# Block-sparse attention: the scores of two heads in one product of 128 rows and 64 columns, queries in five zeroed places read with a stride, heads dealt out anew

## The chip, the cores and the metric

The kernel runs on one core of a Trainium2 chip, as one launch. The metric is the device time of that launch in microseconds (us), the median of several runs. The profile beside it is one execution, recorded by the hardware profiler. In its rows PE is TensorE (matmuls), PEld is TensorE loading the stationary operand of a matmul, DVE is VectorE, ACT is ScalarE, POOL is GpSimd, SP is SyncE, which here only issues transfers (DMAs). A name with a q behind it (SPq, ACTq) is that engine's sequencer. L334 is line 334 of the kernel.

## The reference, cut to what matters

Four batches, eight heads, 768 positions in 24 blocks of 32, 64 numbers a head. All is float32.

```python
scores = (q @ k.T) / 8                     # per batch and head
mask   = |block_i - block_j| <= 1          # the window
mask  |= block_i in (0, 23) or block_j in (0, 23)
mask  |= block_j in sampled_blocks[block_i]   # 3 random blocks for each row of blocks
attn   = softmax(where(mask, scores, -1e9))
x      = attn @ v                          # (4, 768, 512), heads side by side
theta  = x @ w_theta
y      = w_tok_r @ (x * cos(theta)) + w_tok_i @ (x * sin(theta))   # over positions
u      = x + y
out    = u + relu(u @ w_ch)
```

The three sampled blocks are an input and known only at run time.

## The kernel before, in words

**Two stages.** `attention` works through 56 units; `token_mix` (called `follow`) is the rest of the reference, and starts inside the last steps of attention. The change touches attention alone.

**Units.** The batches go in two pairs (`bp`), and one unit handles the 16 heads of a pair (2 batches of 8 heads) for one block of 32 queries. For each pair there are six wide units (`"w"`), which do the first and the last block of queries against all keys, and 22 inner units (blocks 1 to 22), each against eight blocks of 32 keys: the window, the first and last block and the three sampled ones, gathered in `kgs` (keys) and in `vas`, `vbs` (values). So there are 44 inner units.

**A unit's stages**, each a function:

- `scores` (S): products of queries (stationary) and keys (moving) into two PSUM banks, then a VectorE minimum over each row (`m`, L337; the scale is -1/8, so that the minimum is the maximum of the scores). In an inner unit these are 16 products, one a head (L334): each takes 64 rows of the array (the numbers of one head) and 32 columns (its 32 queries), with 256 keys streaming. The head's index is dealt out as `e` (which half of the 128 rows, 2), `p` (which 32 of the 128 columns, 4) and `b` (the batch, 2). Every float32 product is two matmuls with two loads of the stationary operand in the trace, so an inner unit shows 32 matmuls S and 32 loads.
- `weights` (P): four exponentials on ScalarE (L354).
- `turn` (T): eight 128x128 transposes on TensorE (L364); `evict` (pT) copies them to SBUF on ScalarE (L370).
- `values` (X): 32 products of 128 rows and 32 columns with 65 columns of values streaming (the 65th is a column of ones and gives the sum), 64 matmuls in the trace (L388); in a wide unit half as many, of 64 columns (X_w).
- `finish` (DVE): division by the sum; `store` writes two units' outputs to DRAM (`xs`). For wide units `join` (POOL) and `joined` combine the three parts and write them with four DMAs each (L432).

**Order.** It is written out by hand (`tc.manual_schedule()`): in step n each engine gets its instructions in this order: scores(n+1), the keys of n+3 (POOL and ACT: `gather_window`, `gather_keys`, `gather_key`), a share of decoding the token mix's weights (`Decoder`, mostly DVE), turn(n), values(n-1), evict(n), weights(n+1), scale of the queries of n+3 (`scale_q`, ACT), finish(n-1), then the transfers: `load_q` for n+6 (SP), `gather_values` for n+2 (POOL, an indirect DMA, L308), `load_window` for n+1 (SP, and a POOL copy, L299), `store` (SP). TensorE's order in a step is therefore S(n+1), T(n), X(n-1). Queues are worked in order.

**Queries.** `load_q` fetches two units' queries with one DMA of 256 KB into one of four rotating tiles; `scale_q` scales both at once on ScalarE (L239, 512 numbers a row). The decoder's pieces are 512 or 576 numbers wide.

**Heads.** On the host `rows_by_head` puts the two halves `e` of a batch's heads in the upper and lower 64 rows.

Of the kernel before, what the change touches and what calls it, by code (L numbers as in the profile page):

```python
# [10 lines left out]
F32 = mybir.dt.float32  # L11
# [8 lines left out]
P = 128  # L20
NB = 24
NP = 2
ZEROS = float(768 * NP)
Q_BUFS = 4
VB = 4


# [148 lines left out]
def attention(tc, qT, qE, kT, vr, sampled, xs, ident, early_pieces, late_pieces, first_place, follow, spares):  # L176
# [10 lines left out]

    nc = tc.nc  # L190
    with ExitStack() as ctx, ExitStack() as early:

# [6 lines left out]
        qp = ctx.enter_context(tc.tile_pool(name="qp", bufs=1))  # L199
# [10 lines left out]
        ks, wide, qbs, qes, unscaled, st, numbers = {}, {}, {}, {}, {}, {}, {}  # L210
# [15 lines left out]
        def load_wide(bp, t, queue=nc.sync):  # L226
            for c in (2 * t, 2 * t + 1):
                queue.dma_start(wide[bp][c], vr[768 * bp + 128 * c : 768 * bp + 128 * c + 128])

        def load_q(bp, i):  # L230
            if i % 2 == 0:
                return
            t = qp.tile([P, 2, 2, 4, 32], F32, tag="q", name=f"q{bp}_{i}", bufs=Q_BUFS)
            nc.sync.dma_start(t.rearrange("r u b p f -> r u (b p f)"), qT[bp][:, i - 1 : i + 1, :])
            qbs[bp, i], qbs[bp, i + 1] = t[:, 0], t[:, 1]
            unscaled[bp, i] = t.rearrange("r u b p f -> r (u b p f)")

        def scale(tile_):
            nc.scalar.mul(tile_, tile_, -0.125)  # L239

        def scale_q(bp, i):
            if (bp, i) in unscaled:
                scale(unscaled.pop((bp, i)))

        def scale_edges(bp):
            scale(qes[bp].rearrange("r b p f -> r (b p f)"))
# [68 lines left out]
        def scores(unit):  # L315

            bp, i, x = unit
            s = st[unit] = {}
            sc = ps_s[units.index(unit) % 2].tile([P, 2, 2, 256], F32, tag="S", name=f"S{name(unit)}")
            heads = [(b, p, e) for b in range(2) for p in range(4) for e in range(2)]  # L320
            if i == "w":
                t, a = x
                q, keys = qes[bp], ks[bp][:, 8 * t : 8 * t + 8]
                for b, s_, e in [(b, p, e) for b, p, e in heads if p < 2]:
                    rows, p = slice(64 * e, 64 * e + 64), 2 * a + s_
                    nc.tensor.matmul(sc[64 * s_ : 64 * s_ + 64, e, b, :], q[rows, b, p, :], keys[rows, :, 4 * b + p, :], start=True, stop=True)
                if t == 0:
                    mxs[a] = wp.tile([P, 3, 4], F32, tag="mx", name=f"mx{name(unit)}")
                m = mxs[a][:, t]
            else:  # L330
                q, keys = qbs.pop((bp, i)), kgs[i % 2]
                for b, p, e in heads:
                    rows = slice(64 * e, 64 * e + 64)
                    nc.tensor.matmul(sc[32 * p : 32 * p + 32, e, b, :], q[rows, b, p, :], keys[rows, :, 4 * b + p, :], start=True, stop=True)  # L334
# [38 lines left out]
        def values(unit):  # L373
            bp, i, x = unit
            s = st[unit]
            s["X"] = ps_x.tile([P, 2, 2, 65], F32, tag="X", name=f"X{name(unit)}")
            if i == "w":
                t, a = x
                parts, width = [(wide[bp][2 * t + c], 128) for c in range(2)], 64
            else:  # L380
                parts = [(vas[i % 2], 96 if i == 1 else 128), (vbs[(i + 1) % VB], 96 if i == NB - 2 else 128)]
                a, width = 0, 32
            for b in range(2):
                for e in range(2):
                    for c, (v, rows) in enumerate(parts):
                        for w_ in range(128 // width):
                            rr, v0 = slice(width * w_, width * w_ + width), 260 * (2 * b + e) + 65 * (2 * a + w_)
                            nc.tensor.matmul(  # L388
                                s["X"][rr, b, e, :], s["T"][0:rows, 4 * c + 2 * e + b, rr], v[0:rows, v0 : v0 + 65], start=c == 0, stop=c == 1,
                            )  # L390
# [35 lines left out]
        def joined(bp, a):  # L426
            xe = wp.tile([P, 2, 2, 2, 64], F32, tag="xo", name=f"xe{bp}_{a}", bufs=2)[:, 0]
            normalised(f"{bp}_a{a}", xws[a][:, 0], xe)
            for s_ in range(2):
                for z in range(2):  # L430
                    r0, p0 = 64 * s_ + 32 * z, 32 * (2 * a + s_)
                    nc.sync.dma_start(xs[bp, p0 : p0 + 32, (NB - 1) * z].rearrange("r b c -> r (b c)"), xe[r0 : r0 + 32].rearrange("r b e d -> r (b e d)"))  # L432

        mxs, fs, xws, xos = {}, {}, {}, {}
        units = []
# [16 lines left out]

        spares.append(lambda: qp.tile([P, 4, 4, 32], F32, tag="q", name=f"spare{len(spares)}", bufs=Q_BUFS))
        with tc.manual_schedule():
            tab = Tables(nc, cp, sampled)
            load_edges(0)
            make_places(0)
            load_k(0, 0, 8)  # L460

# [5 lines left out]
            for t in range(1, 3):  # L467
                load_k(0, 8 * t, 8)
                load_wide(0, t)
                decoder.load(t - 1, nc.sync)  # L470
                load_q(0, 2 * t - 1)
            make_places(1)
            scale_edges(0)
            do(0, scores)
            do(0, weights)
            steps = len(units) + 1
            for n in range(steps):
# [338 lines left out]
def sparse_attention_then_token_mix(ctx, tc, qT, qE, kT, vr, sampled, w_theta, w_tok_r, w_tok_i, w_ch, outT):  # L816
    nc = tc.nc
    n_batch = outT.shape[0]
# [3 lines left out]
    bias = []  # L822
# [4 lines left out]
    xs = dram.tile([NP, P, NB, 2, P], F32, name="xs")  # L827
# [25 lines left out]
    def pieces(name, f0, f1, f, tiles):  # L853


        def piece(c):
            parts = lambda: [t[:, c - f0 : c - f0 + f] for t in tiles()]
            return Piece(nc, parts, words[name][:, 2 * c : 2 * (c + f)], f"{name}_{c}")
# [10 lines left out]
    late = pieces("tok_r", 2304, 4608, 576, chunks(second, 0, 3)) + pieces("tok_i", 0, 3072, 512, chunks(second, 3, 4))  # L869
# [5 lines left out]
    follow = token_mix(tc, w, last, xs, outT, bias, n_batch, lambda: spares[0]())  # L875
# [50 lines left out]
```

## Time and profile before

| | us |
|---|---|
| three runs | 613.40, 607.53, 612.38 |
| their median | 612.38 |
| the profiled execution: its own time | 617.04 |
| the profiled execution: span from first to last instruction | 615.3 |
| mean granted TensorE clock in it | 0.969 |

A row of the timeline reads: start (us from the span's start), duration, engine, line, operation, output <- input, shape (rows x columns of the array, then the operand), count, and in brackets how long the engine was idle before and what ended it. In the chain of work that ended last a row reads: start, duration, what; "issue" is time in which the engine waited for nothing that the profile shows. A row of the stretches reads: from:to, length, then busy time and number of instructions of PE, PEld, DVE, ACT and POOL, the granted clock, the DMA engines' busy share and GB/s.

### The profile page before, as it was taken

The page shows a single profiled execution, that of the slowest core. Times are in us where ns is not written, and L with a number is a line of the kernel's source. Part 1 is how long each engine was busy: PE and PEld are TensorE (multiplying, and loading weights), DVE is VectorE, ACT ScalarE, POOL GpSimd, SP SyncE. Part 2 cuts the span into 40 slices and gives each one's busy share as a digit, 9 for nine tenths or more (in the row PEclk, how much of TensorE's full clock was granted, in tenths as well). Part 3 has the DMA queues.
Part 4 walks back from the last instruction along what each step waited for, and adds up shares of the span by engine and source line. Part 5 has one row for each costly group of instructions (what it writes and reads, how often), then busy time and mean ns, then how long its engine had stood idle before and what let it go on. Part 6 is the DMA issues. An engine that isn't in the chain of part 4 may idle for free.

```text
span 615.3 us, 17294 instructions
## 1 busy us (share of the span) xinstructions
PE 554.5 (90%) x7072; PEld 437.4 (71%) x7072; DVE 424.5 (69%) x845; ACT 336.2 (55%) x684; POOL 176.4 (29%) x280
## 2 busy tenths in 40 slices
PE   3988769779978886999999997999999999999997
PEld 1755546557645554678888886888888888888886
DVE  5589657768898999787999996456852548723252
ACT  2887658758948877775656553143740446520220
POOL 1399666643596677450000010000000000000000
PEclk9999789998979999999999998999999999999999
DMA  8979996877888889662323132311212210112002
GB/s 307 325 173 258 254 259 203 252 213 256 250 222 231 251 216 269 180 170 85 105 84 105 49 86 69 105 35 34 64 40 78 79 51 22 37 39 77 1 0 103
DMA packets 53199, 86.67 MB, mean 141 GB/s; under 512 B 5504, under 2 KB 31744, under 8 KB 52736
## 3 DMA queue, kind: packets, MB, share of 16 engines
q1 hardware_dynamic: 43440, 54.27, 29.1%
q0 software_dynamic: 6688, 21.78, 13.4%
q10 hardware_dynamic: 2992, 9.51, 5.3%
q8 instruction: 56, 0.92, 0.6%
q14 instruction: 23, 0.19, 0.1%
HBM read 72.95 MB, written 12.58 MB: 139 GB/s over the span
## 4 chain that ended last, share of the span: by engine, by line
PE 64%; DVE 12%; DMA 9%; issue 7%; ACT 6%; SPq 1%; POOL 1%; DVEq 0%; ACTq 0%; POOLq 0%
PE ya L654 14%; PE X L388 8%; PE S L334 7%; PE yb L654 7%; PE T L364 6%; DMA va<-in_vr_dram 5%; PE o L681 2%; PE h L595 2%; PE o L683 2%; PE h L598 2%; PE h L596 2%; PE o L682 2%; PE T_w L364 2%; PE X_w L388 2%; ACT zh L636 2%
## 5 line engine op out<-in xcount | busy, mean ns | idle before, releaser
L654 PE MATMUL ya<-w_second,zh 128*128 128x512 f32 x288 | 107.1, 396 | 0.0
L654 PE MATMUL yb<-w_second,zh 128*128 128x256 f32 x288 | 80.5, 279 | 0.0
L334 PE MATMUL S<-kg,q 64*32 64x256 f32 x1408 | 62.5, 407 | 14.0 <-issue 13.8
L354 ACT ACTIVATE P<-S,m 128x256 f32<-128x256 f32 x176 | 69.6, 492 | 6.7 <-DVE m L337 6.4
L370 ACT COPY pT<-T 128x512 f32<-128x512 f32 x88 | 47.6, 593 | 37.3 <-PE T L364 37.0
L337 DVE TENSOR_REDUCE m<-S 128x4 f32<-128x1024 f32 x44 | 53.7, 1220 | 19.1 <-PE S L334 15.1
L388 PE MATMUL X<-vb,pT 128*32 128x65 f32 (+1 forms) x1408 | 55.6, 231 | 10.7 <-issue 10.0
L654 PEld LDWEIGHTS ya<-w_second,zh 128*128 128x128 f32 x288 | 54.1, 188 | 14.0
L388 PE MATMUL X<-va,pT 128*32 128x65 f32 (+1 forms) x1408 | 50.7, 233 | 11.5 <-issue 6.6
L364 PEld LDWEIGHTS T<-ident,P 128*128 128x128 f32 x352 | 40.9, 148 | 27.2 <-issue 10.7
L364 PE MATMUL T<-ident,P 128*128 128x128 f32 x352 | 55.0, 296 | 4.2 <-issue 3.9
L654 PE MATMUL ya<-w_second,zl 128*128 128x512 f32 x144 | 58.0, 403 | 0.0
L654 PEld LDWEIGHTS yb<-w_second,zh 128*128 128x128 f32 x288 | 54.4, 189 | 0.4
L388 PEld LDWEIGHTS X<-vb,pT 128*32 128x32 f32 (+1 forms) x1408 | 40.3, 117 | 15.8 <-issue 15.7
L388 PEld LDWEIGHTS X<-va,pT 128*32 128x32 f32 (+1 forms) x1408 | 35.7, 115 | 20.6 <-issue 13.8
L334 PEld LDWEIGHTS S<-kg,q 64*32 64x32 f32 x1408 | 25.7, 111 | 32.4 <-issue 24.8
L308 POOL DMA_INDIRECT vb<-in_vr_dram,rows x44 | 43.6, 991 | 17.0 <-PE X_w L388 9.3
L611 DVE SCALAR_TENSOR_TENSOR rr<-t,h 128x512 f32<-128x512 f32 x24 | 16.5, 687 | 36.6 <-ACT t L605 36.6
L654 PE MATMUL yb<-w_second,zl 128*128 128x256 f32 x144 | 40.9, 284 | 0.0
L689 DVE SCALAR_TENSOR_TENSOR of<-o,xT 128x512 f32<-128x512 f32 (+1 forms) x24 | 13.2, 557 | 39.1 <-PE o L683 35.7
L299 POOL COPY va<-va 32x1040 f32<-32x1040 f32 (+1 forms) x28 | 30.4, 1086 | 33.7 <-DMA va<-in_vr_dram 16.2
L595 PE MATMUL h<-w_theta_hi,xh 128*128 128x512 f32 x96 | 38.3, 399 | 0.4 <-ACT xh L584 0.4
(167 smaller groups left out, 1320.2 us busy)
## 6 DMA issues: line engine op xcount, KB each, us to landing
va<-in_vr_dram SPq DMA_DIRECT2D x58, 130.0 KB
q<-in_qT_dram SPq DMA_DIRECT2D x22, 256.0 KB
xs<-xo SPq DMA_DIRECT2D x22, 256.0 KB
xr<-xs SPq DMA_DIRECT2D x22, 256.0 KB
xa<-xs SPq DMA_DIRECT2D x88, 64.0 KB
raw_tok_r<-in_w_tok_r_dram ACTq DMA_DIRECT2D x8, 576.0 KB
out_dram<-of SPq DMA_DIRECT2D x16, 256.0 KB
kv<-in_vr_dram SPq DMA_DIRECT2D x6, 520.0 KB
```

The costliest lines, as they stand in the source:

```text
L299: nc.gpsimd.tensor_copy(va[rows], vas[(i + 1) % 2][rows])
L308: nc.gpsimd.indirect_dma_start(out=vb[0:96], out_offset=None, in_=vr, in_offset=bass.IndirectOffsetOnAxis(ap=tab.rows[:, bp, i : i + 1], a ...
L334: nc.tensor.matmul(sc[32 * p : 32 * p + 32, e, b, :], q[rows, b, p, :], keys[rows, :, 4 * b + p, :], start=True, stop=True)
L337: nc.vector.tensor_reduce(m.rearrange("r (e b) -> r e b", e=2), sc, axis=AX.X, op=ALU.min)
L354: nc.scalar.activation(pt[:, e, b], sc[:, e, b], AF.Exp, bias=m[:, 2 * e + b : 2 * e + b + 1], scale=-1.0)
L364: nc.tensor.transpose(banks[k // 4][:, k % 4], pt[:, (k // 2) % 2, k % 2, 128 * (k // 4) : 128 * (k // 4) + 128], ident)
L370: nc.scalar.copy(out[:, 4 * h : 4 * h + 4], bank)
L388: nc.tensor.matmul(s["X"][rr, b, e, :], s["T"][0:rows, 4 * c + 2 * e + b, rr], v[0:rows, v0 : v0 + 65], start=c == 0, stop=c == 1,)
L595: nc.tensor.matmul(ps, hi[:, c, :], wh[:, c, :], start=c == 0, stop=False)
L611: nc.vector.scalar_tensor_tensor(r, t, -C1, ps, op0=ALU.mult, op1=ALU.add)
L654: nc.tensor.matmul(acc, z[:, dd], wt[:, t0 : t0 + n], start=first and (n == 512 or c % 2 == 0), stop=last, skip_group_check=n == 256,)
L689: nc.vector.scalar_tensor_tensor(o, ps, 0.0, xT[b][:, e : e + groups, t0 : t0 + n], op0=ALU.max, op1=ALU.add)
```

## The change

An inner unit's 16 products of 64 rows and 32 columns become eight of 128 rows and 64 columns, two heads each. The stationary operand holds the two heads' queries block-diagonally: head 0 of the two in the upper 64 rows and the first 32 columns, head 1 in the lower 64 rows and the last 32 columns, zeros elsewhere. For that the queries lie in five fixed places `qs` of 128 x (2, 32, 8) numbers, zeroed once at the start by POOL; a load writes only the non-zero halves (two DMAs of 64 KB for each unit, instead of one of 256 KB for two units), and the stationary operand of a product is read from it with a step of eight numbers. The scale goes over the whole place, so there is one for each unit instead of one for two. The queries of unit n+5 are loaded in step n instead of those of n+6. Keys, the values' products, transposes and exponentials keep their shapes; the heads are dealt out in another order (`r`, which 64 columns, is now outside `s`, which half of the rows), so the joined outputs of the wide units need eight DMAs instead of four. The decoder's pieces of 576 become pieces of 512 with a shorter last one (two pieces more). Two of the five places later serve as the two spare tiles of the token mix, which before came from the rotating ones.

```diff
-Q_BUFS = 4
+NQ = 5
...
+        qs = [qp.tile([P, 2, 32, 8], F32, name=f"q{x}") for x in range(NQ)]
...
+        def q_place(bp, i):
+            return qs[((NB - 2) * bp + i - 1) % NQ]
+
         def load_q(bp, i):
-            if i % 2 == 0:
-                return
-            t = qp.tile([P, 2, 2, 4, 32], F32, tag="q", name=f"q{bp}_{i}", bufs=Q_BUFS)
-            nc.sync.dma_start(t.rearrange("r u b p f -> r u (b p f)"), qT[bp][:, i - 1 : i + 1, :])
...
+            t = q_place(bp, i).rearrange("r s f h -> r s (f h)")
+            for s in range(2):
+                rows = slice(64 * s, 64 * s + 64)
+                nc.sync.dma_start(t[rows, s], qT[bp][rows, i - 1])
...
         def scale_q(bp, i):
-            if (bp, i) in unscaled:
-                scale(unscaled.pop((bp, i)))
+            scale(q_place(bp, i).rearrange("r s f h -> r (s f h)"))
...
-                q, keys = qbs.pop((bp, i)), kgs[i % 2]
-                for b, p, e in heads:
-                    rows = slice(64 * e, 64 * e + 64)
-                    nc.tensor.matmul(sc[32 * p : 32 * p + 32, e, b, :], q[rows, b, p, :], keys[rows, :, 4 * b + p, :], start=True, stop=True)
+                q, keys = q_place(bp, i).rearrange("r s f h -> r h (s f)"), kgs[i % 2]
+                for b, e, r in [(b, e, r) for b in range(2) for e in range(2) for r in range(2)]:
+                    h = 4 * b + 2 * e + r
+                    nc.tensor.matmul(sc[64 * r : 64 * r + 64, e, b, :], q[:, h, :], keys[:, :, h, :], start=True, stop=True)
...
-            for s_ in range(2):
+            for r in range(2):
                 for z in range(2):
-                    r0, p0 = 64 * s_ + 32 * z, 32 * (2 * a + s_)
-                    nc.sync.dma_start(xs[bp, p0 : p0 + 32, (NB - 1) * z].rearrange("r b c -> r (b c)"), xe[r0 : r0 + 32].rearrange("r b e d -> r (b e d)"))
+                    out = xs[bp, 64 * r : 64 * r + 64, (NB - 1) * z, :, 64 * a : 64 * a + 64].rearrange("(s q) b d -> q s b d", s=2)
+                    rows = slice(64 * r + 32 * z, 64 * r + 32 * z + 32)
+                    for s in range(2):
+                        nc.sync.dma_start(out[:, s], xe[rows, :, s])
...
             load_edges(0)
+            for t in qs:
+                nc.gpsimd.memset(t, 0.0)
             make_places(0)
...
                 load_q(0, 2 * t - 1)
+                load_q(0, 2 * t)
...
-                if units[min(n + 6, steps - 2)][:2] not in ((0, 1), (0, 3)):
-                    inner(n + 6, load_q)
+                if units[min(n + 5, steps - 2)][:2] not in [(0, i) for i in range(1, 5)]:
+                    inner(n + 5, load_q)
...
-    early = pieces("theta", 0, 2048, 512, all_of("theta")) + pieces("tok_r", 0, 2304, 576, chunks(lambda: first, 0, 3))
+    early = pieces("theta", 0, 2048, 512, all_of("theta")) + pieces("tok_r", 0, 2304, 512, chunks(lambda: first, 0, 3))
...
-        return np.asarray(a).reshape(NP, 2, 2, 4, NB, 32, 64).transpose(0, 2, 6, 4, 1, 3, 5)
+        return np.asarray(a).reshape(NP, 2, 4, 2, NB, 32, 64).transpose(0, 3, 6, 4, 1, 2, 5)
```

More of the change, by code (lines that the diff above doesn't have):

```diff
@@ L209, in attention @@
         vbs = [gp.tile([P, 1040], F32, name=f"vb{x}") for x in range(VB)]
-        ks, wide, qbs, qes, unscaled, st, numbers = {}, {}, {}, {}, {}, {}, {}
+        qs = [qp.tile([P, 2, 32, 8], F32, name=f"q{x}") for x in range(NQ)]
+        ks, wide, qes, st, numbers = {}, {}, {}, {}, {}
         def make_places(bp):
@@ L228, in load_wide @@
                 queue.dma_start(wide[bp][c], vr[768 * bp + 128 * c : 768 * bp + 128 * c + 128])
+        def q_place(bp, i):
+            return qs[((NB - 2) * bp + i - 1) % NQ]
         def load_q(bp, i):
-            if i % 2 == 0:
-                return
-            t = qp.tile([P, 2, 2, 4, 32], F32, tag="q", name=f"q{bp}_{i}", bufs=Q_BUFS)
-            nc.sync.dma_start(t.rearrange("r u b p f -> r u (b p f)"), qT[bp][:, i - 1 : i + 1, :])
-            qbs[bp, i], qbs[bp, i + 1] = t[:, 0], t[:, 1]
-            unscaled[bp, i] = t.rearrange("r u b p f -> r (u b p f)")
+            t = q_place(bp, i).rearrange("r s f h -> r s (f h)")
+            for s in range(2):
+                rows = slice(64 * s, 64 * s + 64)
+                nc.sync.dma_start(t[rows, s], qT[bp][rows, i - 1])
         def scale(tile_):
@@ L319, in scores @@
             sc = ps_s[units.index(unit) % 2].tile([P, 2, 2, 256], F32, tag="S", name=f"S{name(unit)}")
-            heads = [(b, p, e) for b in range(2) for p in range(4) for e in range(2)]
             if i == "w":
@@ L323, in scores @@
                 q, keys = qes[bp], ks[bp][:, 8 * t : 8 * t + 8]
-                for b, s_, e in [(b, p, e) for b, p, e in heads if p < 2]:
-                    rows, p = slice(64 * e, 64 * e + 64), 2 * a + s_
-                    nc.tensor.matmul(sc[64 * s_ : 64 * s_ + 64, e, b, :], q[rows, b, p, :], keys[rows, :, 4 * b + p, :], start=True, stop=True)
+                for b, r, s_ in [(b, r, s_) for b in range(2) for r in range(2) for s_ in range(2)]:
+                    rows, h = slice(64 * s_, 64 * s_ + 64), 2 * a + r
+                    nc.tensor.matmul(sc[64 * r : 64 * r + 64, s_, b, :], q[rows, b, h, :], keys[rows, :, 4 * b + h, :], start=True, stop=True)
                 if t == 0:
@@ L381, in values @@
                 parts = [(vas[i % 2], 96 if i == 1 else 128), (vbs[(i + 1) % VB], 96 if i == NB - 2 else 128)]
-                a, width = 0, 32
+                width = 32
             for b in range(2):
@@ L386, in values @@
                         for w_ in range(128 // width):
-                            rr, v0 = slice(width * w_, width * w_ + width), 260 * (2 * b + e) + 65 * (2 * a + w_)
+                            rr = slice(width * w_, width * w_ + width)
+                            v0 = 65 * (8 * b + 4 * a + 2 * w_ + e if i == "w" else 8 * b + 4 * e + w_)
                             nc.tensor.matmul(
@@ L450, in inner @@
                 stage(*units[n][:2])
-        spares.append(lambda: qp.tile([P, 4, 4, 32], F32, tag="q", name=f"spare{len(spares)}", bufs=Q_BUFS))
+        spares += [q_place(1, i).rearrange("r s f h -> r (s f h)").rearrange("r (i c f) -> r i c f", i=4, c=4) for i in (NB - 6, NB - 5)]
         with tc.manual_schedule():
@@ L856, in piece @@
         def piece(c):
-            parts = lambda: [t[:, c - f0 : c - f0 + f] for t in tiles()]
-            return Piece(nc, parts, words[name][:, 2 * c : 2 * (c + f)], f"{name}_{c}")
+            c1 = min(c + f, f1)
+            parts = lambda: [t[:, c - f0 : c1 - f0] for t in tiles()]
+            return Piece(nc, parts, words[name][:, 2 * c : 2 * c1], f"{name}_{c}")
         return [piece(c) for c in range(f0, f1, f)]
@@ L866, in chunks @@
         return lambda: [tile_()[:, x, 768 * at : 768 * (at + n)] for x in range(2)]
-    early = pieces("theta", 0, 2048, 512, all_of("theta")) + pieces("tok_r", 0, 2304, 576, chunks(lambda: first, 0, 3))
-    late = pieces("tok_r", 2304, 4608, 576, chunks(second, 0, 3)) + pieces("tok_i", 0, 3072, 512, chunks(second, 3, 4))
+    early = pieces("theta", 0, 2048, 512, all_of("theta")) + pieces("tok_r", 0, 2304, 512, chunks(lambda: first, 0, 3))
+    late = pieces("tok_r", 2304, 4608, 512, chunks(second, 0, 3)) + pieces("tok_i", 0, 3072, 512, chunks(second, 3, 4))
     def last():
@@ L874, in sparse_attention_then_token_mix @@
     spares = []
-    follow = token_mix(tc, w, last, xs, outT, bias, n_batch, lambda: spares[0]())
+    follow = token_mix(tc, w, last, xs, outT, bias, n_batch, lambda: spares.pop(0))
     attention(tc, qT, qE, kT, vr, sampled.bitcast(I32), xs, ident, early, late, first_place, follow, spares)
@@ L903 @@
     arrays = {
-        "qT": np.ascontiguousarray(qh[:, :, :, 1:-1]).reshape(NP, P, NB - 2, 256),
+        "qT": np.ascontiguousarray(qh[:, :, :, 1:-1].transpose(0, 1, 2, 3, 6, 4, 5)).reshape(NP, P, NB - 2, 256),
         "qE": np.ascontiguousarray(qh[:, :, :, [0, NB - 1]].transpose(0, 1, 2, 4, 5, 3, 6)).reshape(NP, P, 512),
```

## The prediction, written before the changed kernel was run

> **What bounds the kernel now.** I read the page first, then the chain of work that ended last, in order of time.
>
> ```profile
> PE   3988769779978886999999997999999999999997
> PE 64%; DVE 12%; DMA 9%; issue 7%; ACT 6%; SPq 1%; POOL 1%; DVEq 0%; ACTq 0%; POOLq 0%
> 30.30:265.90 235.60, 194.37 (x4837) 133.32 (x4830) 190.87 (x338) 175.01 (x407) 158.13 (x238) 0.93 0.84 233
> ```
>
> The slices show two stages. From about 270 us on TensorE is full; that is the token mix, which the change leaves alone. Before it lies attention. The last row is its stretch with inner units, 235.6 us: no engine is full, DVE with 191 us nearly as busy as TensorE with 194, and the DMA engines at 0.84. So what ends last must be read from single steps:
>
> ```profile
> 100.08 1.02 PE T L364 x8
> 101.11 1.04 PE X L388 x64
> 102.15 0.91 PE S L334 x12
> 103.06 0.10 issue
> 103.16 1.08 PE S L334 x20
> 104.24 1.02 PE T L364 x8
> 105.26 0.93 PE X L388 x56
> 106.19 0.21 issue
> 106.40 0.29 PE X L388 x3
> 106.69 0.42 issue
> 107.11 0.33 PE X L388 x5
> 107.44 1.02 PE S L334 x32
> 108.47 1.02 PE T L364 x8
> ```
>
> Two whole steps lie on TensorE alone: T to T 4.16 and 4.23 us. T, X and S at their best are 1.02 + 1.04 + 1.02 = 3.08, so about 1.1 us a step is TensorE waiting for nothing that the profile names: in the second step in the last eighth of X, in the first inside S. GpSimd's rows show what runs then:
>
> ```profile
> 101.80 1.26 POOL L308 DMA_INDIRECT vb<-in_vr_dram,rows  x1 [0.15 <-issue]
> 105.82 0.96 POOL L308 DMA_INDIRECT vb<-in_vr_dram,rows  x1 [0.15 <-issue]
> ```
>
> In both steps TensorE's matmuls resume about 0.55 us after the start of the indirect transfer, and again 1.3 us after it (106.40 and 107.11 against 105.82; 103.16 against 101.80). I take it that TensorE gets no new instructions while GpSimd makes the descriptors, and lives on what it has queued; X eats that up (64 matmuls and 64 loads in 1.04 us). I call it the freeze.
>
> The second kind of wait is longer:
>
> ```profile
> 57.22:65.62 8.40, 5.04 (x125) 3.49 (x126) 7.36 (x11) 7.38 (x17) 7.32 (x11) 0.94 1.04 258
> 65.62:89.48 23.86, 18.86 (x506) 13.09 (x505) 14.21 (x28) 14.21 (x33) 14.78 (x22) 0.86 0.93 248
> q8 instruction: 56, 0.92, 0.6%
> 33.08 1.52 issue
> ...
> 62.75 2.87 issue
> ...
> 67.58 1.89 PE S L334 x32
> ...
> 242.07 2.22 issue
> ```
>
> I cut the stretches at the ends of long "issue" waits. Matmuls and loads between them: 251 and 1011, that is one and four times about 252. The instruction queue moved 56 packets and 0.92 MB, 16 KB each. So TensorE's instructions come in blocks of some 252, and a long wait stands only at the start of a block: the next one had not landed while the DMA engines were at 0.93 to 1.04. The chain has eleven such waits over 1.1 us (first 33.08, last 242.07), together 22.8 us. After the longest ones the granted clock falls too (0.86 in the second stretch): the S behind the wait at 62.75 takes 1.89 us instead of 1.02.
>
> **The Trainium skill** speaks against this reading: "Runtime: NRT & Kernel Launch", section Instruction fetch mechanics, says that crossing a 16 KiB boundary is mostly hidden. The trace agrees on the blocks and differs on the cost, as the counts above show. By the page alone the third term below would be nothing, and the sum 631.
>
> **The change, part by part.**
>
> *Array time of S.*
>
> ```profile
> 18.85 1.08 PE X_w L388 x32
> 19.94 1.02 PE S_w L326 x16
> ```
>
> S on 64x32 places (eight at once) does 32 matmuls in 1.02 us (107.44), S_w on 64x64 (four at once) 16 in 1.02: four rounds each. X_w uses 128x64, as the new S does, and does 32 matmuls in 1.08, where X on 128x32 (four at once) does 64 in 1.04: 16 rounds each, so two such places work at once and their loads hide. The new S has 16 matmuls on two places: eight rounds, twice the streaming. If the low clock behind 62.75 is half the full one, 1.89 against 1.02 (107.44) splits S into 0.87 of streaming and 0.15 fixed. So the new S takes 2 x 0.87 + 0.15 = 1.89, that is **+0.87 us in each of 44 units, +38.3 us** if nothing covers it. The bounds: 0 if steps were set elsewhere, +38.3 with no cover.
>
> *What the freeze gives back.* S now has 32 instructions for 1.89 us instead of 64 for 1.02, so a queue that carried S for 0.4 us carries it for 1.6. Where the freeze falls in S (the step at 100.08) the longer S runs through it: 1.02 + 1.04 + about 0.3 + 1.89 = 4.25, no loss. Where it falls in X (104.24) nothing is covered: 1.02 + 2.18 + 1.89 = 5.09. The indirect transfer follows the gathers of keys, which wait for the end of S, so its place against T and X does not move. Of some 30 steps without a long wait I count half of either kind: 15 x 0.8 = **-12 us**. Bounds: 0 and -25.
>
> *Fewer instructions.* A step goes from 208 matmuls and loads to 176, and lasts about 4.75 instead of 4.2 us: a block of 252 lasts 6.8 instead of 5.1. Each long wait shrinks by about 1.6 us or goes. Of the 22.8 us on the chain those over 1.6 (3.52, 2.87, 2.81, 2.44, 2.22, 2.12) leave 6.4, so -16.4; but five steps that hid their freeze in such a wait then show it, +4: **-12.4 us**. Bounds: 0 and -22.8.
>
> *The clock.* S at the low clock costs 0.87 more; T and X as much again each, if they stretch alike, so such a step loses 2.6. The trace has four behind waits of about 3 us. Three go: **-8 us**. Where one stays, S there takes 4 x 0.87 + 0.15 = 3.6.
>
> *Transfers on SP.*
>
> ```profile
> q<-in_qT_dram SPq DMA_DIRECT2D x22, 256.0 KB
> xs<-xe SPq DMA_DIRECT2D x16, 32.0 KB
> 46.83 0.41 SPq L432
> ...
> 49.83 4.52 DMA va<-in_vr_dram
> SPq L302 <- PE X L388: 105.3, 37, 7.7
> SPq L432 <- DMA q<-in_qT_dram: 2.9, 1, 2.9
> ```
>
> The joined outputs go from 16 issues to 32, in two places. Behind them on SP waits the load of `va`, for which X waits: the chain runs through L432 into it (46.83 to 49.83). Eight more issues at 0.41 are 3.3 us a place, 6.6 in both; half of it is hidden, as each place is two steps long: **+3.5 us**, bounds 0 and +6.6, without waits for landings (a rival, below). The queries go from 22 issues to 88 with the same bytes, one and a half more a step at some 0.4 us; on SP that lies in the 105 us in which it waits for X anyway (2.8 us a time). Longer steps give every `va` more time: of the waits for `va` on the chain (the 4.52 at 49.83 is one) I take off 3, an estimate: **-3 us**, bounds 0 and -10.
>
> *The rest, at nothing.*
>
> ```profile
> L239 ACT ACTIVATE q<-q 128x512 f32<-128x512 f32 x22 | 14.9, 677 | 0.0
> ACT pT L370 <- PE T L364: 37.0, 30, 5.0
> 0.75 0.20 POOL masks.py:197 MEMSET ident<- 128x128 f32 x1 [0.29 <-POOLq L914]
> ```
>
> 22 more scales of 0.677 are 14.9 us of ScalarE, half of them in steps that had one already; it idles 37 us before pT, waiting for T. Without that cover: +15. Five zeroings of 512 columns are 5 x 4 x 0.2 = 4 us on GpSimd, which then has nothing else to do until the first keys land; without that cover +4. Two more pieces of the decoder move the same numbers. The spare tiles wait for S of their unit, which stands earlier in the same step.
>
> Sum: 38.3 - 12 - 12.4 - 8 + 3.5 - 3 = **+6.4 us**. On the profiled execution (617.04; span 615.3 and 1.7 around it) that gives 623.4. That execution is 4.7 over the median of the three runs (612.38); on the median the forecast is **619**.
>
> **The rivals.**
>
> *Faster: the freeze and the blocks give nearly all back.* If the indirect transfer slips behind X in nearly all steps (a window copy of two parts before it is enough: 100.08), the second term is -25 instead of -12, and with every long wait gone the third is up to -19. That gives 619 - 13 - 6 = 600, and I say 602. For it: the undisturbed steps show 4.16 and 4.23 whichever way the freeze falls, so it is the freeze that sets them, not TensorE's sum. Against it: the gathers' order is kept.
>
> *Slower: the transfers' turns.* The row of L432 waiting 2.9 us for a load of queries shows that an issue may have to wait for an unrelated earlier transfer to land; so the number in flight is limited, and the change adds 66 issues of queries and 16 of joined outputs. Landing takes 4.5 us in the `va` row, more than a step. It decides when SP's wait reaches over the 2.8 us that it spends waiting for X: if one in four of the 66 costs 1 us at X, +16: 635. Against it: the transfers are short, and SP has the slack.
>
> *Slower: the step of eight numbers.* A round of X_w hides two loads of 64 columns in 1.08 / 16 = 0.068 us; a round of S lasts 0.87 / 4 = 0.22. So loads may be three times slower for nothing; at four times a round takes 0.27, S +0.4 and the kernel +18: 637; at eight times 730. No row shows such a load. The Trainium skill, "SBUF — State Buffer", section Door 1: The DMA port swizzle, has accesses that leave a 16-byte line each time pay a penalty, with four float32 numbers as the free step; eight is over it. It names no factor, and no run here shows one.
>
> That the change does not do what it says (two heads in one product) I leave out; the shapes leave no other way.
>
> **How the numbers follow.** The forecast of 619 (with its own bounds about 610 to 630) has 0.45, the faster rival 0.27, the transfers 0.22, the slow loads 0.06. About 1%, 6 us, is what a measurement can tell from no change, so 606 and 618.5 are the borders. Faster: three quarters of the first rival, 0.20. The same: the rest of it and less than half of the forecast, 0.28. Slower: 0.52. The range 600 to 640 leaves out less than half of the faster rival (0.11) and the loads' upper half and the transfers' tail (0.08).
>
> **What would show it.** S in the changed profile: 16 x 44 matmuls of 128x64, from S to the next T 1.89 us; 1.02 would overthrow the first term, over 2 the loads' speed is at work. Steps of two kinds, near 4.25 and 5.1 us; if all are near 4.2, the faster rival holds. The stretches between long "issue" waits still count 252, with fewer and shorter waits and fewer stretches at half clock; waits as long as before overthrow the third and fourth terms. On SP, waits of L234, L302 and L432 for landings grow from a few us to tens if the transfers' turns decide. What would make the prediction wrong most easily is the second term: where GpSimd's descriptors fall.

## The result, and the profile after

The changed kernel takes 630.31 us (median of four runs, 625.24 to 631.68), the kernel before 610.68 on the same chip. The ratio is **1.0297, 95% interval 1.0225 to 1.037**: slower by about 18 us. The ratios here and below leave out runs that fell in a slower state of the chip, so they can differ from the quotient of two medians. The forecast was 619, inside a range of 600 to 640. The sign was right; the size was 11 us short.

The two profiled executions are not of equal rank. That of before (617.04) lies above the four timed runs beside it (the highest 613.4), that of the changed kernel (625.24) is the fastest of its four. Between them lie only 8.2 us. The rows below show which way each term went; they can't show the whole 18.

The page of the changed kernel, the slices of TensorE, the instruction queue, the shares of the chain and the groups of S and T; behind it, in a fence of its own, the stretch of attention by windows:

```profile
PE   3997897899978899999999996999999999999997
...
q8 instruction: 50, 0.82, 0.6%
...
PE 75%; DMA 10%; DVE 7%; ACT 3%; issue 2%; SPq 1%; POOL 1%; DVEq 0%; ACTq 0%
...
L335 PE MATMUL S<-kg,q 128*64 128x256 f32 x704 | 92.9, 404 | 4.4 <-DMA va<-in_vr_dram 2.7
...
L365 PE MATMUL T<-ident,P 128*128 128x128 f32 x352 | 51.5, 285 | 3.0 <-ACT P L355 2.7
```

```profile
28.00:281.37 253.37, 226.52 (x4355) 180.19 (x4353) 195.98 (x374) 195.21 (x452) 161.19 (x239) 0.97 0.85 224
```

The same window and groups in the kernel before:

```profile
28.00:275.02 247.02, 205.36 (x5055) 141.81 (x5053) 200.53 (x361) 185.79 (x427) 161.45 (x242) 0.93 0.82 228
```

```profile
L334 PE MATMUL S<-kg,q 64*32 64x256 f32 x1408 | 62.5, 407 | 14.0 <-issue 13.8
...
L364 PE MATMUL T<-ident,P 128*128 128x128 f32 x352 | 55.0, 296 | 4.2 <-issue 3.9
```

Both windows end at the first product `ya` of the token mix; three groups of its products `h` lie inside both. By these windows attention is 6.35 us longer: TensorE's matmuls (the first sum behind the stretch) went from 205.4 to 226.5, its idle time, the rest of the stretch, from 41.7 to 26.9. S alone rose by 30.4. The idle time by what ended it, TensorE's waits in the window of before:

```profile
PE X L388 <- issue: 16.7, 28, 2.9
PE S L334 <- issue: 13.8, 10, 3.5
PE X L388 <- DMA va<-in_vr_dram: 4.2, 5, 2.2
PE T L364 <- issue: 3.9, 3, 3.4
```

and of the changed kernel:

```profile
PE X L390 <- issue: 7.4, 18, 1.1
PE X L390 <- DMA va<-in_vr_dram: 4.4, 4, 2.5
PE S L335 <- DMA va<-in_vr_dram: 2.7, 1, 2.7
PE T L365 <- ACT P L355: 2.7, 3, 2.1
PE X L390 <- DVE w_second L85: 2.6, 1, 2.6
```

The columns are the total, the count and the longest. Waits that no other engine ended ("issue") fell from 34.4 us to 8.5, 7.4 of them in the row shown; the longest from 3.5 to 1.1. The long ones went: TensorE's timeline has eleven over 1.1 us in the kernel before, 23.9 us together, and none in the changed one; the shorter ones fell from 10.8 to 8.4. On the chain their share fell from 7% to 2%, and the instruction queue moved 50 blocks instead of 56. In their place stand values that had not landed (4.2 to 7.1), exponentials and VectorE.

Two kinds of steps are left, from the chain of work:

```profile
105.48 1.03 PE X L390 x61
106.52 0.13 issue
106.64 0.27 PE X L390 x2
106.92 0.48 issue
107.39 0.23 PE X L390
107.62 1.94 PE S L335 x16
...
228.21 1.04 PE X L390 x64
229.25 1.94 PE S L335 x16
231.19 1.02 PE T L365 x8
```

and GpSimd's indirect transfers in those two steps, from its timeline:

```profile
106.12 0.94 POOL L310 DMA_INDIRECT vb<-in_vr_dram,rows  x1 [0.16 <-issue]
...
230.60 1.19 POOL L310 DMA_INDIRECT vb<-in_vr_dram,rows  x1 [0.16 <-issue]
```

The descriptors that begin 0.64 us after X (106.12) stretch it from 1.04 to 2.14 us (105.48 to 107.62). Those that begin inside the long S (230.60) cost nothing. Of the 43 distances from one T to the next, 14 are 4.25 us or less and 14 lie between 4.9 and 5.2: the two kinds of steps that the prediction asked for.

### The profile page after: what moved, and what is told of

It is laid out like the page before. It is cut to its first block, busy times and chain, and to the rows that moved or that the text cites. A ratio compares the mean times of both kernels' runs of the same rounds, so it can differ in the third digit from the quotient of the medians.

```text
span 623.5 us, 16136 instructions
## 1 busy us (share of the span) xinstructions
PE 575.8 (92%) x6368; PEld 476.0 (76%) x6368; DVE 420.6 (67%) x859; ACT 346.8 (56%) x710; POOL 180.9 (29%) x285
## 4 chain that ended last, share of the span: by engine, by line
PE 75%; DMA 10%; DVE 7%; ACT 3%; issue 2%; SPq 1%; POOL 1%; DVEq 0%; ACTq 0%
PE ya L661 20%; PE yb L661 10%; PE S L335 10%; PE X L390 6%; PE T L365 5%; DMA va<-in_vr_dram 5%; PE h L602 3%; PE h L605 3%; PE h L603 3%; PE o L688 3%; PE o L689 3%; PE o L690 3%; PE T_w L365 2%; DMA xa<-xs 1%; PE S_w L327 1%
## 5 line engine op out<-in xcount | busy, mean ns | idle before, releaser
L335 PE MATMUL S<-kg,q 128*64 128x256 f32 x704 | 92.9, 404 | 4.4 <-DMA va<-in_vr_dram 2.7
L335 PEld LDWEIGHTS S<-kg,q 128*64 128x64 f32 x704 | 69.7, 200 | 13.8 <-issue 6.4
L355 ACT ACTIVATE P<-S,m 128x256 f32<-128x256 f32 x176 | 69.8, 497 | 11.7 <-DVE m L338 10.4
L371 ACT COPY pT<-T 128x512 f32<-128x512 f32 x88 | 47.7, 600 | 30.6 <-PE T L365 30.4
L390 PE MATMUL X<-va,pT 128*32 128x65 f32 (+1 forms) x1408 | 48.8, 226 | 11.1 <-DMA va<-in_vr_dram 4.4
L390 PE MATMUL X<-vb,pT 128*32 128x65 f32 (+1 forms) x1408 | 49.5, 224 | 5.8 <-issue 5.4
L365 PEld LDWEIGHTS T<-ident,P 128*128 128x128 f32 x352 | 38.9, 143 | 20.2 <-ACT P L355 8.9
L365 PE MATMUL T<-ident,P 128*128 128x128 f32 x352 | 51.5, 285 | 3.0 <-ACT P L355 2.7
L390 PEld LDWEIGHTS X<-vb,pT 128*32 128x32 f32 (+1 forms) x1408 | 37.2, 112 | 10.0 <-issue 9.7
L696 DVE SCALAR_TENSOR_TENSOR of<-o,xT 128x512 f32<-128x512 f32 (+1 forms) x24 | 13.2, 557 | 38.9 <-PE o L690 35.5
```

Source lines behind the costliest of these rows:

```text
L335: nc.tensor.matmul(sc[64 * r : 64 * r + 64, e, b, :], q[:, h, :], keys[:, :, h, :], start=True, stop=True)
L355: nc.scalar.activation(pt[:, e, b], sc[:, e, b], AF.Exp, bias=m[:, 2 * e + b : 2 * e + b + 1], scale=-1.0)
L365: nc.tensor.transpose(banks[k // 4][:, k % 4], pt[:, (k // 2) % 2, k % 2, 128 * (k // 4) : 128 * (k // 4) + 128], ident)
L371: nc.scalar.copy(out[:, 4 * h : 4 * h + 4], bank)
L390: nc.tensor.matmul(s["X"][rr, b, e, :], s["T"][0:rows, 4 * c + 2 * e + b, rr], v[0:rows, v0 : v0 + 65], start=c == 0, stop=c == 1,)
```

## The experiments

Each ratio is to the kernel before, run on the same chip in the same rounds, with its 95% interval.

**e1: the array places of the change, the instruction count of before.** Each product is cut in two of 128 keys.

```diff
-  nc.tensor.matmul(sc[64 * r : 64 * r + 64, e, b, :], q[:, h, :], keys[:, :, h, :], start=True, stop=True)
+  for z in range(2):
+      nc.tensor.matmul(sc[64 * r : 64 * r + 64, e, b, 128 * z : 128 * z + 128], q[:, h, :], keys[:, 4 * z : 4 * z + 4, h, :], start=True, stop=True)
```

> The changed kernel with each product cut into two of 128 keys: 32 matmuls and 32 loads for S in an inner unit, as before the change, on the same two places of the array. Theory A (array time costs, fewer instructions give part of it back): the long waits for blocks of instructions return, over 15 us of them on TensorE instead of 8; S stays at 1.9 us if the loads hide behind 128 columns; time 8 to 20 us over the changed kernel, ratio to before 1.04 to 1.06. Theory B (the transfers on SP hold up va): as the changed kernel, 1.03, within 3 us.

Measured: 643.85 us, **1.0596 (1.0519 to 1.0672)**. The time is as Theory A had it, but not for its reason: S did not stay at 1.9 us, and few of the waits for instructions returned. The chain of this kernel:

```profile
231.16 1.04 PE X L391 x64
232.20 2.26 PE S L336 x32
```

S takes 2.26 us here instead of 1.94: 44 x 0.32 = 14 us, most of the distance to the changed kernel (0.03 of 611, 18 us). TensorE's "issue" waits rose only from 8.5 to 13.2 us (11.7 at X and 1.5 at S), far from the 34.4 of before. With steps of 4.3 us and more, 64 instructions in S are delivered nearly in time.

**e2: the array time of before, the instruction count of the change.** Products of 64 rows and 64 columns, four at once; half of the contraction is left out.

```diff
-  nc.tensor.matmul(sc[64 * r : 64 * r + 64, e, b, :], q[:, h, :], keys[:, :, h, :], start=True, stop=True)
+  rows = slice(64 * e, 64 * e + 64)
+  nc.tensor.matmul(sc[64 * r : 64 * r + 64, e, b, :], q[rows, h, :], keys[rows, :, h, :], start=True, stop=True)
```

> The changed kernel with products of 64 rows and 64 columns: half of the contraction is left out, so half of the heads get no scores. Instructions and transfers of the changed kernel, array time of S as before (four places at once, 1.02 us). Theory A: 44 x 0.9 = 40 us of array time go, the part that the freeze had hidden (about 12) comes back, so 20 to 30 us under the changed kernel: 600 to 610, ratio 0.98 to 1.00. Theory B: va arrives as late as in the changed kernel, so at most 8 us are gained: 622 or more, ratio 1.02 or more.

Measured: 619.88 us, **1.0200 (1.012 to 1.0281)**. Theory A is wrong on this: with S back at 1.09 us the kernel is still 12 us slower than before, and only some 6 us are won of the 38. TensorE's waits in attention:

```profile
PE X L391 <- DMA va<-in_vr_dram: 17.1, 8, 3.7
PE X L391 <- issue: 7.3, 14, 1.4
PE T L366 <- ACT P L356: 7.0, 6, 2.9
PE S L336 <- issue: 3.9, 4, 2.7
```

"Issue" is 11.2 us, a third of before: fewer instructions do take most of these waits away with S as short as before, and three steps in a row take 3.15, 3.15 and 3.62 us. (Other waits lengthen other steps, which gives the delivery more time too.) But the time goes to the next in line: values not landed 17.1 us (4.2 before), and exponentials 7.0 (before has no such row of its own).

**e3 and e4: the loads of queries.** e3 loads the queries of a unit with one transfer of 128 rows instead of two of 64 (the zero places are then lost). e4 loads only the first five units' queries.

```diff
-  for s in range(2):
-      rows = slice(64 * s, 64 * s + 64)
-      nc.sync.dma_start(t[rows, s], qT[bp][rows, i - 1])
+  nc.sync.dma_start(t[:, 0], qT[bp][:, i - 1])      # e3

+  if bp or i > NQ:                                  # e4, ahead of the loads
+      return
```

> The changed kernel with one load of queries for each unit, 128 rows into the first half of its place, instead of two of 64 rows: the same bytes, 44 issues instead of 88; the block diagonal is lost, so the scores are others. Theory A: within 4 us of the changed kernel, ratio 1.025 to 1.035. Theory B: half of what the transfers cost is gone: 5 to 8 us faster, 1.017 to 1.022, and SP's waits for X (55 us in the changed kernel, 105 before) grow by 15 or more.

> The changed kernel with only the first five units' queries loaded: 78 of the 88 loads of queries are left out (5 MB), and the later units use old queries. Theory A: within 6 us of the changed kernel, the small gain coming from 5 MB less in the transfer engines. Theory B: 12 to 20 us faster, ratio 1.00 to 1.01, and SP's waits for X back at about 100 us.

Measured: e3 623.87 us, **1.0279 (1.0199 to 1.0358)**; e4 621.07 us, **1.0223 (1.0147 to 1.0299)**. Halving the issues changes nothing that can be told in the time. On SP it changes much: its waits for X are 85.7 us in e3 and 55.5 in the changed kernel, its waits for landings 3.7 and 22.4. That is Theory B's sign without its gain in time. Dropping the loads wins perhaps 4.5 us (0.0074 of 611), within the intervals. So Theory B alone can't carry the 18 us either.

**e11: the loads of queries the other way round,** in the kernel before, each cut into four.

```diff
-  nc.sync.dma_start(t.rearrange("r u b p f -> r u (b p f)"), qT[bp][:, i - 1 : i + 1, :])
+  for u in range(2):
+      for s in range(2):
+          rows = slice(64 * s, 64 * s + 64)
+          nc.sync.dma_start(t[rows, u].rearrange("r b p f -> r (b p f)"), qT[bp][rows, i - 1 + u])
```

> The kernel before with each load of queries of two units cut into four transfers of 64 KB, so 88 issues of queries instead of 22, of the same bytes. The prediction (hidden in the time that SP waits for X anyway): 0.995 to 1.005. The rival (the transfers' turns): 1.015 to 1.03.

Measured: 616.87 us, **1.0116 (1.0074 to 1.0159)**: 88 issues instead of 22 cost some 7 us. The prediction had nothing, the rival 9 us or more; the result lies between the two. SP's waits show where:

```profile
SPq L305 <- PE X L391: 62.4, 30, 8.5
...
SPq L305 <- DMA raw_tok_r<-in_w_tok_r_dram: 8.6, 3, 3.8
```

L305 issues the load of `va`. It waited three times for the landing of a transfer of the decoder that has nothing to do with it, up to 3.8 us. All such waits of SP for landings are 20.9 us in this kernel, 7.6 before, 22.4 in the changed kernel and 3.5 in e4 (sums over the rows). The slack in front of `va` (waits for X) is 62.4 us instead of 105.3.

**e5: the joined outputs,** written by four transfers as before (the blocks at both ends are misplaced).

```diff
-  for s in range(2):
-      nc.sync.dma_start(out[:, s], xe[rows, :, s])
+  nc.sync.dma_start(xs[bp, p0 : p0 + 32, (NB - 1) * z].rearrange("r b c -> r (b c)"), xe[r0 : r0 + 32].rearrange("r b e d -> r (b e d)"))
```

> The changed kernel with the joined outputs of the wide units written by four transfers as before instead of eight (the blocks at the two ends of each sequence are then misplaced). The prediction's term: 3.5 us less, at most 6.6, so a ratio to the kernel before of 1.018 to 1.026. The rival that an issue waits its turn behind earlier transfers: 8 us or more less, 1.01 to 1.016. If the extra issues are hidden: as the changed kernel, 1.026 to 1.034.

Measured: 618.57 us (five runs, 615.25 to 625.46), **1.0100 (1.0029 to 1.0172)**: 12 us less than the changed kernel, by medians that scatter. The ratio lies at the low end of the rival's range, outside the prediction's. One part can be seen. Behind the first place the load of `va` on which the chain hangs is issued at 60.97 us in the changed kernel:

```profile
60.97 8.06 DMA va<-in_vr_dram
```

and 3.7 us earlier in e5:

```profile
57.24 7.78 DMA va<-in_vr_dram
```

Behind the second place e5 is 1.0 us further ahead (by the starts of T). That is 4.7 us, the prediction's 3.5 and a little; at the first product of the token mix 1.3 of them are left in these two executions. What the 12 of the medians are made of, the profiles don't show.

**e8 and e9: no descriptors.** In either kernel the indirect transfer becomes a plain one of the same size on SP; the random choice of values is left out.

```diff
-  nc.gpsimd.indirect_dma_start(out=vb[0:96], out_offset=None, in_=vr, in_offset=...)
+  nc.sync.dma_start(vb[0:96], vr[768 * bp + 32 * i : 768 * bp + 32 * i + 96])
```

> The kernel before with the indirect transfer replaced by a plain transfer of 96 rows in a row, of the same size, issued on SP: the random choice of values is left out, the rest is the same. Theory A: without descriptors on GpSimd TensorE loses about 1.1 us less in each of 44 steps; VectorE and ScalarE then set the steps near 3.6 to 3.8 us, 15 to 30 us in all: 0.95 to 0.975. Theory B: the bytes are the same and SP gets one issue more a step: 0.99 to 1.02.

> The changed kernel with the same plain transfer in place of the indirect one. Theory A: the steps fall from 4.2 and 5.1 us to about 4.0 (1.02 + 1.04 + 1.89), 20 to 28 us in all: 0.985 to 1.00 of the kernel before, and some 20 us behind the kernel before without the indirect transfer, which is the array time of S that nothing covers. Theory B: 1.02 to 1.04, as the changed kernel.

Measured: e8 611.72 us, **0.9984 (0.9947 to 1.0020)**; e9 616.55 us, **1.0117 (1.0066 to 1.0168)**. The same exchange is worth nothing in the kernel before and 11 us in the changed one (1.0297 - 1.0117). Theory A missed with both; it had e9 some 20 us behind e8, and it is 4.8. The chain of e8 shows a part of why:

```profile
101.81 1.02 PE T L359 x8
102.83 1.28 PE X L383 x64
104.11 1.02 PE S L329 x32
105.13 1.02 PE T L359 x8
...
107.77 2.12 issue
```

The stop is gone: T to T is 3.32 us here, and 3.03 to 3.10 in three other steps between 70 and 120 us, where the kernel before has none under 4.09. But in the next step the instructions are late by 2 us. TensorE's waits in e8:

```profile
PE X L383 <- issue: 16.2, 14, 2.7
PE S L329 <- issue: 10.9, 7, 2.6
PE T L359 <- ACT P L349: 7.2, 6, 2.4
PE X L383 <- DMA va<-in_vr_dram: 6.7, 3, 3.1
```

"Issue" is still 28 us, 6 less than before. The long waits have stayed: eleven over 1.1 us, 21.2 us together, against eleven and 23.9. Waits for P and `va` are 13.9 us instead of 4.2. So the stop is gone, but the steps now end on late instructions, exponentials and values.

The two runs change one more thing: SP gets 44 more issues. Its waits for landings are 19.7 us in e8 (7.6 before) and 42.3 in e9 (22.4 in the changed kernel), and e11 put 66 more issues at 7 us. Part of what the missing stop wins may be lost there, in e8 and in e9; no run parts the two. In e9, from the timeline of TensorE, S begins at

```profile
109.09 2.01 PE L330 MATMUL S<-kg,q 128*64 128x256 f32 x16
...
113.10 2.01 PE L330 MATMUL S<-kg,q 128*64 128x256 f32 x16
```

4.01 us apart, and many steps of e9 are 4.01 to the hundredth: TensorE alone sets them. Its "issue" waits at X are 2.3 us; what is left is mainly `va`, 11.7, and exponentials, 5.4.

**e6, e7 and e10: where the descriptors fall.** The gather of sampled values is moved ahead of the gathers of keys: in e6 in the changed kernel, in e7 in the kernel before, in e10 in the changed kernel for the inner units from the seventh block on.

```diff
+  inner(n + 2, gather_values)                 # e6, e7; e10: only for i > 6
   inner(n + 3, gather_window)
...
-  inner(n + 2, gather_values)                 # e10: only for i <= 6
```

> The changed kernel with the gather of a step's sampled values issued ahead of the gathers of keys of that step instead of behind the scaling of queries, so that GpSimd makes the descriptors early in the step, beside the long S. Theory A (TensorE gets no new instructions while the descriptors are made, and only a long S covers that): the steps of 5.1 us become steps of 4.2 to 4.3, some 20 times 0.8 us: 612 to 618 us, ratio to the kernel before 1.00 to 1.015. Theory B (transfers: the loads of va and of queries, and their landings, set the steps): the move changes nothing of them, 1.025 to 1.04.

> The kernel before with the same move of the gather of sampled values. Theory A: S of 1.02 us holds 64 instructions and covers no more of the freeze than X does, so the steps stay near 4.2: 0.985 to 1.01. Theory B: no change, 0.995 to 1.01; so this run tells only whether the move is worth something without the long S. A gain over 1.5% would say that where the descriptors fall matters in the kernel before as well.

> The changed kernel with the gather of sampled values issued ahead of the gathers of keys, for the units from the seventh block of queries on alone (the first six, whose buffers the wide units use, stay where they were). Theory C (the stop of TensorE under the descriptors is fully paid in the changed kernel wherever it falls in X, since nothing else is late there): the steps of 5.0 to 5.2 us of these units become 4.0 to 4.4 and the time comes near that of the changed kernel without the indirect transfer: 614 to 620 us, ratio to the kernel before 1.005 to 1.018. Theory A (the stop was already paid half, and something else is late behind it): 1.022 to 1.035, with waits for va or P in the place of the stop.

In e6 and e7 the move refills buffers that a wide unit still has to read, so some units get values meant for others; in e10 the result is that of the reference. Measured: e6 632.14 us, **1.0265 (1.0182 to 1.0348)**; e7 620.47 us, **1.0123 (1.0057 to 1.0188)**. e6 lies in Theory B's range, e7 above both. They miss Theory A for a reason outside it: at the wide units X_w now waits for those buffers, in e6

```profile
PE X_w L390 <- DMA vb<-in_vr_dram,rows: 9.2, 2, 6.1
```

and 10.0 us in e7. e10 leaves these places alone: 620.80 us, **1.0198 (1.0137 to 1.0259)**, some 6 us better than the changed kernel, between what the theories gave. From its timelines, one such transfer and the S around it:

```profile
199.19 0.93 POOL L310 DMA_INDIRECT vb<-in_vr_dram,rows  x1 [0.16 <-PE S L338]
```

```profile
201.08 2.01 PE L338 MATMUL S<-kg,q 128*64 128x256 f32 x16
...
205.09 2.01 PE L338 MATMUL S<-kg,q 128*64 128x256 f32 x16
```

The descriptors now begin 0.8 us before X (199.19; X from 200.03), and the step is 4.01. So the place decides, as the second term assumed; but not all steps got there, and waits for `va` grew to 9.5 us. It is the best form of the change that was run with the reference's result, and still slower than the kernel before.

**e12: a second scale,** by one, in the kernel before, in each unit that had none.

```diff
+  else:
+      again = unscaled.pop((bp, i - 1))
+      nc.scalar.mul(again, again, 1.0)
```

> The kernel before with a second scale of the same size, by one, in each of the units that had none, so 44 scales instead of 22. The prediction (hidden in the time that ScalarE waits for TensorE): 0.997 to 1.005. If ScalarE is late in the short steps: up to 15 us, 1.01 to 1.025.

Measured: 628.83 us, **1.0306 (1.0249 to 1.0363)**. This run does not tell what it was made for. The tile holds two units' queries, and the first of them is read by the S that comes next. ScalarE's and the chain's rows:

```profile
199.36 0.67 ACT L246 ACTIVATE q<-q 128x512 f32<-128x512 f32 x1
```

```profile
198.11 2.02 issue
200.13 1.10 PE S L337 x32
```

S starts 0.1 us after the end of the scale (200.03), having stood for 2 us: I had added a wait. In the changed kernel a unit's scale is due a whole step ahead of its S. What the 22 extra scales cost stays open; among TensorE's waits in the changed kernel's attention there is no row for an inner unit's q.

## Why the prediction was right and wrong, step by step

**Array time, +38.3: right as a price for each step.** Steps that TensorE alone sets are 4.01 us with the new S (e9) and 3.1 with the old one (e8): 0.9 x 44 = 40. In the time of the whole kernel far less of it shows, because other waits fill the room: 6 us in e2, and 4.8 between e8 and e9. The loads with a stride are slower, as the changed kernel's loads for S and for X_w show (minimum, median, maximum in ns), both 128 rows and 64 columns:

```profile
L335 PEld LDWEIGHTS S<-kg,q x704: 194/196/231, 29.6 to 265.1; 128*64 128x64 f32 x176
```

```profile
L390 PEld LDWEIGHTS X_w<-vb,pT_w x192: 132/138/138, 150.9 to 170.0; 128*64 128x64 f32 x192
```

X_w streams 65 columns and S 256, but this is not the reason: S_w, with 64 rows, 64 columns and 256 streaming, loads in 133 ns without a stride, and the S of e2, of the same shape, in 194 with it. But at 1.4 times the time the loads are hidden, all but some 0.05 us a step (1.94 against the 1.89 forecast); the rival of slow loads is out. The Trainium skill, "SBUF — State Buffer", section Door 1: The DMA port swizzle, has a penalty for leaving a 16-byte line each time and gives no factor; the trace agrees, with 1.4 for eight float32 numbers. That the row of S rose by 30.4 only has two reasons: part of the S of before ran at the low clock, and part was stretched by the stop (62.5 us, and 56.3 in e8 at nearly the same clock).

**Fewer instructions, -12.4: the mechanism right, the size too small.** "Issue" waits fell by 26 us, 23.9 of them the long ones that the term was about. In e2 the lower count does most of it with a short S (11.2 us left); in e1 longer steps do most of it with the old count (13.2 left). The Trainium skill, "Runtime: NRT & Kernel Launch", section Instruction fetch mechanics, has the crossing of a block mostly hidden. That fits the changed kernel, with no wait over 1.1 us, and not the kernel before or e8, with eleven each (23.9 and 21.2 us).

**The freeze, -12: the steps as told, the gain in time not shown.** The stop is there (e8, e9), a long S covers it (230.60; e10), and about as many steps were covered as not, as assumed. The weak place is the next step of the working: I took what S covers as a gain of its own, besides the gain of fewer waits for instructions. e8 shows no gain in the kernel before when the stop goes, because late instructions, exponentials and values then hold the steps up. In the changed kernel, where instructions are in time, the same exchange wins 11 us (e9). Taken at their word, the two runs put the net cost of the stop at 0 before and 11 us after, where the sum had it fall by 12; but both carry SP's extra issues. TensorE's own rows give a third figure: without the stop, S, X and the waits for instructions up to 1.1 us are together 16.0 us shorter in e8 and 13.2 in e9, so by these pairs of executions the long S covered some 3 us, not 12. (S: 62.5 and 56.3, 92.9 and 90.3; X: 63.4 and 56.3, 57.6 and 53.1; the waits: 10.8 and 8.1, 8.4 and 2.3.) What the term was worth stays open.

**The clock, -8: about right.** The granted clock in the window rose from 0.93 to 0.97; T became 3.5 us shorter (55.0 to 51.5), four times the 0.87 of a step at the low clock, where three had been taken. X became 5.8 us shorter (63.4 to 57.6), but a part of that is the stop.

**Joined outputs, +3.5: too small,** 4.7 in the profiles; by the runs 12 with a wide interval, as the rival had it. **Queries, nothing: wrong,** about 5 (e4, within its interval) to 7 us (e11). SP does wait for unrelated landings, as the rival of the transfers' turns told, but the price is less than half of its 16; and e3, which takes these waits away, wins nothing that can be told, so that they are the cost is not shown. **Time for `va`, -3: wrong in sign.** TensorE's waits for `va` rose from 4.2 to 7.1 us. They are 2.7 in e4, without the loads of queries, and 2.5 in e5, with fewer joined outputs.

**The sum and the basis.** Between the two profiled executions the sum held: 6.35 us in attention against 6.4. It held in part by luck: the instruction waits gave more than their term, the freeze by TensorE's rows less, and values, exponentials and VectorE, at -3 or nothing in the sum, took it back. But I moved the result to the median by taking 4.7 us off, as if the changed kernel's profiled execution would lie as far above its median as that of before. It lay 5 below. About 11 us of the 18 to 20 are differences between executions that no profile here shows, and they stay unexplained.

The gains of the single removals (e2 6, e4 4.5, e5 12, e9 11 us) come to 34, nearly twice the loss. They overlap: each opens time that the next wait can fill. So no account that adds up to 18 is claimed. Shown is that the array time is a full 0.9 us a step where TensorE sets the step, that the long instruction waits are gone, and that the stop of TensorE stretches single steps. That the stop, the extra loads of queries and the extra joined outputs each cost time in the changed kernel is likely by e9, e10, e4, e11 and e5, with wide intervals.

## What to carry to other kernels

- Two stalls that fill the same slack can't be counted as two gains. Before a stall is booked as something to be given back, ask what would be late without it. Removing it in the kernel before (here e8, no change) answers that in one run, if nothing else changes with it; here SP got 44 more issues.
- Filling the contraction with zeros to halve the instructions can pay only while the delivery of instructions sets the steps; the price in array time falls due in every step that TensorE sets. Many small transfers are not free on a queue with slack, as e11 shows, where issues wait for earlier landings.
- A profile is one execution; place it among the runs of its own kernel before a difference of two profiles is read as a difference of two kernels.

## What the runs showed of the hardware that was not expected

- TensorE's stop under GpSimd's descriptors depends on where they begin: 0.64 us after the start of X costs it 1.1 us (105.48 to 107.62), 0.8 us before it costs nothing (199.19), and inside an S of 1.94 us nothing (230.60).
- With the stop gone, the kernel before has steps of 3.0 to 3.3 us only one at a time, eight of 43; behind one of them instructions are late by 2.1 us (107.77).
- The load of 64 float32 columns with a stride of eight numbers takes 196 ns at 128 rows, and 194 at 64 rows (e2), so the number of rows made no difference; without the stride it takes 133 (S_w, 64 rows).
